# PE fillers on a tile of ones written by DVE, and the fp32 identity copied by DVE instead of ACT

## The chip, the cores and the metric

The kernel runs on one core of a Trainium2 chip. A core has a matrix engine (PE, TensorE), with its weight loads (PEld) shown apart, a vector engine (DVE), a scalar engine (ACT), a general engine (POOL), which also issues most loads here, and a queue engine (SP), which issues the stores. Each engine runs its own instructions in order and waits for others by semaphores. The metric is the device time of one execution in microseconds; the median of several runs is compared.

## What is computed

Chunked attention, followed by a two-layer network with a leaky ReLU, over 8 batches, 8 heads, 576 positions and a head size of 64:

```python
chunk = 64
scores = scale * np.matmul(q_c, k_c.transpose(0, 1, 2, 4, 3))   # per chunk of 64
scores = scores - np.max(scores, axis=-1, keepdims=True)
attn = np.exp(scores)
attn = attn / (np.sum(attn, axis=-1, keepdims=True) + 1e-09)
out = np.matmul(attn, v_c)
...
x = np.ascontiguousarray(attn_out.transpose(0, 2, 1, 3)).reshape(B * S, H * D)   # 4608 x 512
h = x @ w_in                    # 512 -> 2048
g = np.maximum(0.01 * h, h)
out = (g @ w_out)               # 2048 -> 512, float32
```

Inputs and output are fp32 in memory; the kernel computes its matmuls in fp16, but for the first transposes.

## The kernel before

Work is cut into units of 128 token positions (two chunks), 36 in all; unit u covers 8 heads at once. For a unit, the stages have one letter each: `tq` and `tk` transpose queries and keys on PE into PSUM (L259), `q` and `k` copy them to SBUF (L272 or L274 into the tile QZ, which holds the two head halves in zeroed blocks; L279 or L281 into KT), `s` computes the scores (L309), `m` and `b` find and subtract the maximum (DVE), `x` takes the exponential (ACT, L328), `z` and `n` sum and normalise (DVE), `e` transposes the result on PE (L351), `c` copies it, `v` multiplies by the values (L376) with the tile VB, whose unused blocks are zeroed, and `a` stores the unit's 512 features per token in xT (ACT, L389). From unit 9 on, transposes are done by DVE and by DMA instead.

The network takes xT in blocks of tokens (BLOCKS, L46; the first six are of 128). First layer: `mm1` (L157) and ACT's `act1` (L172); second layer: `mm2` (L182), ACT's copy (L193) and a store from SP (L195).

The order of everything is the order of the program text, which each engine follows for its own instructions. Up to unit 5 it is a list written out by hand, FRONT (L431), whose words name a stage and its arguments. Besides the stages above, its words are `y` (DVE zeroes a QZ tile, 0 to 2, or one half of a VB tile, from 3 up, L417), `w` (ACT zeroes a VB half in two steps, L424), `I` (the identity is copied to fp32, L410), `i` with a number (that many filler matmuls, whose results nobody reads, into a PSUM tile of the matmul pool, L396), `A`, `G`, `B`, `O` (first layer, its activation, second layer, store, of the first blocks). After FRONT a loop (L473) runs the stages of unit `it` and its neighbours between `fill` calls, which take matmuls of the network from a list.

Loads are issued up front by POOL in the order of LOADS (L133): `g` are a unit's queries and keys (L69), `v` values (L96), `Q` quarters of the first weights (L103), `P` quarters of the second (L115), `D` a whole batch of queries and keys for the later units (L87). POOL makes the fp16 identity after the first of these, `g1` (a memset and a select, masks.py:197 and 199). The queries and keys of unit 0, q_f and k_f, are loaded in fp32 by SP and ACT (L123). They are fp32 in SBUF, so unit 0's two transposes use the fp32 identity, `ident32`; all others use the fp16 `ident`. Each DMA load is spread over 16 DMA engines, and PE, in order, cannot pass a transpose whose load hasn't landed.

DVE's first writes are two columns, `one` (which ACT reads for a first exponential behind its table load, L127) and `zeros` (which ACT's zeroing reads).

Of the kernel before, what the change touches and what calls it, by code (L numbers as in the profile page):

```python
# [8 lines left out]
FP16 = mybir.dt.float16  # L9
FP32 = mybir.dt.float32  # L10
ALU = mybir.AluOpType
AFT = mybir.ActivationFunctionType
# [4 lines left out]
def kernel(  # L17
# [9 lines left out]
    nc = tc.nc  # L27
# [20 lines left out]
    sbp = ctx.enter_context(tc.tile_pool(name="k_sb", bufs=1))  # L48
# [72 lines left out]
    for eng, name, src in ((nc.sync, "q_f", q), (nc.scalar, "k_f", k)):  # L121
        t = sbp.tile([128, H, D], FP32, name=name)
        eng.dma_start(out=t, in_=src[0, :, 0:G, :].rearrange("h p d -> p h d"))  # L123
        first.append(t)
    one = sbp.tile([128, 1], FP16, name="one")
    nc.vector.memset(one, 0.0)
    nc.scalar.activation(out=one, in_=one, func=AFT.Exp, bias=0.0, scale=1.0)  # L127
# [8 lines left out]
    ident = sbp.tile([128, 128], FP16, name="ident")  # L136
# [4 lines left out]
    ident32 = sbp.tile([128, 128], FP32, name="ident32")  # L141
# [251 lines left out]
    def idle(n):  # L393
        t = psp.tile([128, 4, 128], FP32, name="idle", tag="mm", bufs=4)
        for i in range(n):
            nc.tensor.matmul(out=t[:, i % 4, :], lhsT=ident, rhs=ident, start=True, stop=True)  # L396

    def first_layer(j, a):
        chunks.remove(("mm1", j, a, 0))
# [7 lines left out]
        store(j, 0)  # L407

    def identity():
        nc.scalar.activation(out=ident32, in_=ident, func=AFT.Copy, bias=0.0, scale=1.0)  # L410

    def empty(i):
        i, m = divmod(i, 2)
# [5 lines left out]
    def zero_act(i):  # L419
# [8 lines left out]
            )  # L428

    FRONT = (  # L430
        "y0 y1 y2 y4 w3 I y5 i12 tq0 tk0 q0.1.1 q0.0 tq1 k0.1 q1.0.1 i4 s0 tk1 m0 k1 b0 q1.1.1 i23 s1 x0 "  # L431
        "m1 b1 z0 x1 z1 i55 tq2 q2.0.1 n0 i7 tk2 k2 q2.1 i3 e0 n1 c0.1 s2 m2 i3 v0 a0 b2 i12 e1 x2 c1 i9 "
        "v1 z2 A0.0 a1 A1.0 n2 G0.0 e2 A0.1 c2 v2 tq3 a2 A1.1 q3.1 G0.1 q3.0 tk3 A2.0 G1.0 k3.1 G1.1 s3 "
        "A0.2 G2.0 m3 A1.2 b3 x3 A2.1 G0.2 z3 A0.3 G1.2 tq4 G2.1 n3 A1.3 G0.3 e3 G1.3 A2.2 c3 q4.0.1 v3 "
# [4 lines left out]
        "tq": stage_tq, "tk": stage_tk, "q": stage_q, "k": stage_k, "s": stage_s, "m": stage_m, "b": stage_b,  # L439
        "x": stage_x, "z": stage_z, "n": stage_n, "e": stage_e, "c": stage_c, "v": stage_v, "a": stage_a, "d": stage_d,  # L440
        "A": first_layer, "G": act1, "B": second_layer, "O": finish, "i": idle, "y": zero, "w": zero_act,
        "I": identity,
    }
    done = set()
# [13 lines left out]
    for what in FRONT.split():  # L458
        name = what.rstrip("0123456789.")
# [80 lines left out]
```

## Time and profile before

| What | us |
|---|---|
| median of 3 runs | 293.99 (293.66 to 294.13) |
| the profiled execution, own time | 294.1 |
| its span, first to last instruction | 292.3 |
| PE busy | 284.4 (97%) |
| DVE busy | 182.7 (63%) |
| ACT busy | 152.5 (52%) |
| POOL busy | 119.4 (41%) |
| fillers (L396), 128 matmuls, busy | 9.6 |
| first filler | 3.80 |
| first matmul of the first layer | 18.57 |

The span runs from the first to the last instruction of the program; 1.8 us of the execution's time lie around it. A chain of waits is followed back from the last instruction: at each step to what released it, or else to the instruction before it on its engine. In the timeline each row has start, duration, engine, line, operation, names and shapes, and in brackets the engine's idle time before it and what ended that. In the list of DMA issues the last number is the median time from issue to landing. PE's busy time counts matmuls whose ends are modelled, so two neighbouring rows overlap; the spacing of starts is what one matmul costs in a stream. The page's row of the granted clock shows full speed in all slices.

### The profile page before, as it was taken

The numbers are of one execution on the slowest core, as the hardware profiler recorded it, in microseconds if no ns is written. First come the engines' busy times: TensorE is split into PE (matmuls) and PEld (weight loads), VectorE is DVE, ScalarE is ACT, GpSimd is POOL, SyncE is SP. The second block draws the span as 40 slices with busy tenths as digits, with TensorE's granted clock in tenths as the row PEclk, the third lists the DMA queues.
The fourth block names the chain that finished last, engine by engine and source line by source line (L and its number), as shares of the span: only waits on it lengthen the run. The fifth ranks groups of instructions, "written<-read, shape, count | busy, mean of one in ns | idle before, by whom it ended". The sixth has DMA issues, their size and how long they took to land.

```text
span 292.3 us, 6210 instructions
## 1 busy us (share of the span) xinstructions
PE 284.4 (97%) x2556; PEld 181.8 (62%) x2556; DVE 182.7 (63%) x338; ACT 152.5 (52%) x270; POOL 119.4 (41%) x148
## 2 busy tenths in 40 slices
PE   4999999999999999999999999999999999999995
PEld 3989955878677766767676754444454444444444
DVE  5776536879899898888877888787777720000000
ACT  5457713756456545646454547733763387127511
POOL 8857547898509837920394379210000000000000
PEclk9999999999999999999999999999999999999999
DMA  9999999999999999999499999992111320120022
GB/s 131 162 193 194 202 157 184 168 144 146 127 126 61 148 147 135 139 132 99 66 135 138 105 85 148 94 137 90 56 23 31 112 69 0 38 88 21 0 74 72
DMA packets 192332, 32.00 MB, mean 109 GB/s; under 512 B 183472, under 2 KB 187824, under 8 KB 192304
## 3 DMA queue, kind: packets, MB, share of 16 engines
q0 software_dynamic: 170208, 18.10, 114.0%
q1 hardware_dynamic: 21056, 13.24, 19.4%
q8 instruction: 20, 0.33, 0.4%
q10 hardware_dynamic: 1040, 0.26, 0.4%
q14 instruction: 8, 0.07, 0.1%
HBM read 36.70 MB, written 9.44 MB: 158 GB/s over the span
## 4 chain that ended last, share of the span: by engine, by line
PE 97%; POOL 1%; ACT 1%; issue 1%; DVE 0%; POOLq 0%
PE hT L157 43%; PE oP L182 41%; PE Sp L309 3%; PE xp L376 3%; PE idle L396 3%; PE oP L203 1%; PE qp L259 1%; PE tpe L351 1%; PE kp L259 1%; POOL k_in L69 0%; DVE QZ L274 0%; ACT KT L281 0%; ACT QZ L272 0%; POOL q_in L69 0%; ACT osb L211 0%
## 5 line engine op out<-in xcount | busy, mean ns | idle before, releaser
L157 PE MATMUL hT<-xT,w_inT 128*128 128x128 f16 (+2 forms) x1152 | 134.3, 273 | 0.0
L182 PE MATMUL oP<-w_outT,gT 128*128 128x512 f16 x560 | 128.2, 379 | 0.0
L157 PEld LDWEIGHTS <-w_inT 128*128 128x128 f16 x1152 | 90.0, 98 | 32.7
L172 ACT ACTIVATE gT<-hT 128x512 f16<-128x512 f32 x144 | 83.8, 597 | 32.5 <-PE hT L157 32.3
L182 PEld LDWEIGHTS <-gT 128*128 128x128 f16 x560 | 52.3, 98 | 56.3
L193 ACT ACTIVATE osb<-oP 128x512 f32<-128x512 f32 x35 | 20.9, 596 | 64.6 <-PE oP L182 62.7
L87 POOL DMA_DIRECT2D q_d<-in_q_dram x48 | 38.7, 818 | 35.3 <-DVE QZ L291 31.6
L318 DVE TENSOR_REDUCE mx<-Sp 128x8 f32<-128x512 f32 x36 | 24.9, 691 | 31.0 <-PE Sp L309 30.8
L87 POOL DMA_DIRECT2D k_d<-in_k_dram x48 | 38.7, 817 | 2.1 <-DMA q_d<-in_q_dram 1.1
L291 DVE STREAM_TRANSPOSE QZ<-q_d 64x512 f16<-64x512 f16 (+1 forms) x60 | 38.2, 644 | 0.4
L389 ACT ACTIVATE xT<-xp 128x512 f16<-128x512 f32 x36 | 21.4, 594 | 20.6 <-PE xp L376 20.6
L96 POOL DMA_DIRECT2D VB<-in_v_dram x16 | 18.4, 1159 | 20.8 <-PE xp L376 20.5
L334 DVE TENSOR_REDUCE z<-ex 128x8 f32<-128x512 f16 x36 | 23.6, 654 | 4.7 <-ACT ex L328 4.6
L322 DVE TENSOR_TENSOR sh<-Sp,mx 128x512 f32<-128x512 f32 x36 | 24.9, 691 | 1.2
L343 DVE TENSOR_TENSOR en<-ex,zi 128x512 f16<-128x512 f16 x36 | 24.8, 690 | 1.2
L328 ACT ACTIVATE ex<-sh 128x512 f16<-128x512 f32 x36 | 22.6, 628 | 5.3 <-DVE sh L322 5.3
L299 DVE STREAM_TRANSPOSE KT<-k_d 128x512 f16<-128x512 f16 (+1 forms) x30 | 19.4, 654 | 0.8
L376 PEld LDWEIGHTS <-VB 128*128 128x128 f16 x288 | 13.1, 98 | 5.6
L309 PEld LDWEIGHTS <-QZ 128*128 128x128 f16 x288 | 13.2, 99 | 5.4 <-DVE QZ L274 0.2
L309 PE MATMUL Sp<-KT,QZ 128*128 128x64 f16 x288 | 14.5, 195 | 0.1
L376 PE MATMUL xp<-et,VB 128*128 128x64 f16 x288 | 14.3, 193 | 0.0
L396 PE MATMUL idle<-ident 128*128 128x128 f16 x128 | 9.6, 233 | 3.8 <-POOL ident masks.py:199 3.8
(42 smaller groups left out, 104.2 us busy)
## 6 DMA issues: line engine op xcount, KB each, us to landing
out_dram<-osb SPq DMA_DIRECT2D x35, 256.0 KB, 2.3
VB<-in_v_dram POOLq DMA_DIRECT2D x16, 288.0 KB, 6.0
q_d<-in_q_dram POOLq DMA_DIRECT2D x48, 72.0 KB, 6.0
k_d<-in_k_dram POOLq DMA_DIRECT2D x48, 72.0 KB, 5.3
w_inT<-in_moe_w_in_dram POOLq DMA_DIRECT2D x8, 256.0 KB, 9.2
w_outT<-in_moe_w_out_dram POOLq DMA_DIRECT2D x4, 512.0 KB, 9.5
q_in<-in_q_dram POOLq DMA_DIRECT2D x7, 128.0 KB, 9.7
k_in<-in_k_dram POOLq DMA_DIRECT2D x7, 128.0 KB, 9.0
```

The costliest lines, as they stand in the source:

```text
L87: nc.gpsimd.dma_start(out=t[p0:p0 + 32, m, :, :, :].rearrange("p h b d -> p (h b) d"), in_=src[b, h0:h0 + 2, :, dh * 32:dh * 32 + 32].rear ...
L157: nc.tensor.matmul(out=hT[:, i, :], lhsT=w_inT[:, t, fc * 128:(fc + 1) * 128], rhs=xT[:, t, r0:r0 + tb], start=(t == 0), stop=(t == NT - 1),)
L172: nc.scalar.activation(out=gT[j][:, nf * a:nf * a + nf, :], in_=HT.pop((j, a)), func=AFT.Prelu, bias=0.0, scale=1.0, alpha=0.01)
L182: nc.tensor.matmul(out=o, lhsT=gT[j][:, fc, ti * 128:(ti + 1) * 128], rhs=w_outT[:, fc, :], start=(n == 0 and fc == part * 4), stop=(n == ...
L291: nc.vector.transpose(out=qz[s * CH:(s + 1) * CH, :, e0:e0 + n, s, :], in_=qkd[b][0][s * CH:(s + 1) * CH, :, at:at + n * CH].rearrange("p ...
L309: nc.tensor.matmul(out=Sp[:, i, :], lhsT=qz[:, 2 * m + g, e, :, :], rhs=kt[:, 2 * m + g, e, :], start=True, stop=True)
L318: nc.vector.tensor_reduce(out=MX[u], in_=SP[u], axis=AXL.X, op=ALU.max)
L322: nc.vector.tensor_tensor(out=SH[u], in0=SP.pop(u), in1=MX.pop(u).unsqueeze(2).to_broadcast((128, 8, CH)), op=ALU.subtract)
L328: nc.scalar.activation(out=E[u], in_=SH.pop(u), func=AFT.Exp, bias=0.0, scale=SCL)
L334: nc.vector.tensor_reduce(out=z, in_=E[u], axis=AXL.X, op=ALU.add)
L343: nc.vector.tensor_tensor(out=E[u], in0=ex, in1=ZI.pop(u).unsqueeze(2).to_broadcast((128, 8, CH)), op=ALU.mult)
L376: nc.tensor.matmul(out=xp[:, t, e, :], lhsT=VB[b % NVB][:, t, c, :], rhs=et[:, t // 2, e, t % 2, :] if u < UD else et[:, t % 2, e, t // 2, :],
```

## The change

A new fp16 tile of 128x128, `warm`, is set to 1.0 by DVE before its other writes, and all fillers use it as weights and as data. The list FRONT begins with 33 fillers; the 12 that stood behind `y5` are gone, the others stay. The copy of the identity to fp32 is done by DVE, behind `y4`, and ACT's zeroing `w3` follows it in the list.

```diff
+    warm = sbp.tile([128, 128], FP16, name="warm")
+    nc.vector.memset(warm, 1.0)
     one = sbp.tile([128, 1], FP16, name="one")
     nc.vector.memset(one, 0.0)
     nc.scalar.activation(out=one, in_=one, func=AFT.Exp, bias=0.0, scale=1.0)
...
     def idle(n):
         t = psp.tile([128, 4, 128], FP32, name="idle", tag="mm", bufs=4)
         for i in range(n):
-            nc.tensor.matmul(out=t[:, i % 4, :], lhsT=ident, rhs=ident, start=True, stop=True)
+            nc.tensor.matmul(out=t[:, i % 4, :], lhsT=warm, rhs=warm, start=True, stop=True)
...
     def identity():
-        nc.scalar.activation(out=ident32, in_=ident, func=AFT.Copy, bias=0.0, scale=1.0)
+        nc.vector.tensor_copy(out=ident32, in_=ident)
...
     FRONT = (
-        "y0 y1 y2 y4 w3 I y5 i12 tq0 tk0 q0.1.1 q0.0 tq1 k0.1 q1.0.1 i4 s0 tk1 m0 k1 b0 q1.1.1 i23 s1 x0 "
+        "i33 y0 y1 y2 y4 I w3 y5 tq0 tk0 q0.1.1 q0.0 tq1 k0.1 q1.0.1 i4 s0 tk1 m0 k1 b0 q1.1.1 i23 s1 x0 "
```

On DVE the order is then `warm`, `one`, `zeros`, three QZ tiles, a VB half, the identity's copy, a VB half, and from there as before. On ACT the copy is missing and the rest stands as it was. PE has 21 weight loads and 21 matmuls more, all at its head.

## The prediction

> **What bounds the kernel now.** I read the page first, then the chain of waits from 0 to 60 us, the waits of PE, the timeline of the first 27 us and of 40.5 to 47.5 us, and the landings of single loads. Times are microseconds from the start of the span.
>
> ```profile
> PE 97%; POOL 1%; ACT 1%; issue 1%; DVE 0%; POOLq 0%
> ```
>
> The chain that ended last is PE almost throughout. The chain of the front shows what fills it before the first layer starts at 18.5:
>
> ```profile
> 3.80 1.46 PE idle L396 x12
> 5.26 0.98 PE qp L259 x4
> 6.24 0.02 issue
> 6.26 0.60 ACT QZ L272
> 6.86 0.02 issue
> 6.88 0.69 DVE QZ L274
> 7.58 0.04 issue
> 7.62 0.59 PE qp L259 x4
> 8.20 0.43 PE idle L396 x4
> 8.63 0.43 PE Sp L309 x8
> 9.06 0.43 PE kp L259 x4
> 9.48 1.39 PE idle L396 x23
> 10.87 0.31 PE Sp L309 x8
> 11.18 3.07 PE idle L396 x55
> ```
>
> Two things are to be seen. First, the start hangs on the identity, and then on its fp32 copy behind ACT's zeroing. Second, the same filler costs 0.43/4 = 0.107 us at 8.2 but 3.07/55 = 0.056 us at 11.2: PE runs at half rate at first. Single matmuls in the trace change spacing at 9.55. From 18.3 on no PE gap exceeds 0.02 us, so a microsecond saved before 18.5 is saved at the end, unless something that PE does not pace is late. In the timeline:
>
> ```profile
> 2.82 1.02 DVE L417 MEMSET VB<- 64x1152 uint32 x1 [0.28 <-issue]
> ...
> 3.45 0.29 POOL masks.py:199 TENSOR_SCALAR_AFFINE_SELECT ident<-ident 128x128 f16<-128x128 f16 x1
> ...
> 4.76 0.29 ACT L410 ACTIVATE ident<-ident 128x128 f32<-128x128 f16 x1
> ```
>
> The order there is POOL's identity, DVE's zeroing of one VB half, ACT's copy of the identity. Later, from the other timeline:
>
> ```profile
> 46.74 0.27 PEld L259 LDWEIGHTS <-k_in 128*128 128x128 f16 x4
> ```
>
> That is the weight load of unit 6's keys. The transfer that brings them was issued at 32.83, and that of the first queries, q_f, at 0.74; the last column is the time from issue to landing:
>
> ```profile
> k_in<-in_k_dram POOLq DMA_DIRECT2D x1, 128.0 KB, 13.5
> ```
>
> ```profile
> q_f<-in_q_dram SPq DMA_DIRECT2D x1, 256.0 KB, 3.9
> ```
>
> So q_f lands at 4.61 and unit 6's keys at 46.33, 0.41 before PE uses them.
>
> **The change part by part.**
>
> *The ones tile.* DVE's first write, now 128x128 fp16. Bounds: 0.06 (the 128x1 memset) and 0.49 (one QZ memset, 128x512 uint32); linear in elements between them gives 0.17. It starts at 0.81 and ends at 0.98, and PE may start at 1.04 (the first filler followed the identity by 0.06). What stands behind it on DVE moves by 0.17: `one` is awaited by ACT only after its table load at 2.54, and the zeroed QZ tiles not before 5.8, so this costs nothing.
>
> *Fillers 12 to 33.* At half rate 33 x 0.107 = 3.52: from 1.04 to 4.56. Before, twelve ended issuing at 5.05. The other fillers keep number and cost, and read ones instead of the identity.
>
> *The fp32 copy.* ACT loses 0.29. DVE does it after the VB memset, which now ends at 3.84 + 0.17 = 4.01; the identity is there at 3.74. The price on DVE isn't in the trace: at least 0.17 (128x8 fp32 TENSOR_SCALAR), at most 0.67 (128x512 cast of KT from fp32); I take 0.30, nearest to ACT's 0.29 for this very tile. It is ready at about 4.35, by the bounds 4.2 to 4.75. Behind it waits the second VB memset, which now ends near 5.6; DVE next works at 6.4. Nothing waits. No DMA is added; POOL's and SP's queues keep their order, and POOL's loads to unit 8 wait for other loads only.
>
> *The first transpose* then waits for the latest of fillers (4.56), copy (4.41 with 0.06 to start) and q_f (4.61 + 0.06 = 4.67). So it starts at 4.67 instead of 5.11: 0.44 gained, set by q_f. With the copy at 0.67 the gain is 0.3.
>
> *Full rate earlier.* Before, it took 9.55 - 3.80 = 5.75 from the first filler. The same interval from 1.04 gives 6.8. The chain from first transpose to the second pair's (L259 at 7.62) took 2.51, in ACT and DVE mostly, so that pair comes at 7.18, already at full rate. Step by step: KT's copy ends at 8.17 - 0.44 = 7.73, and s0 starts at 7.78 (before 8.42, held back by four slow fillers). Eight Sp and four kp matmuls then need 0.62 instead of 1.06, so kp is done at 8.40. ACT's KT (0.60) and QZ half (0.59) end at 9.64, and s1 starts at 9.69 instead of 10.77: 1.08 gained. The 23 fillers end at 9.52 and don't hold it. The 55 fillers at 0.056 follow unchanged, and q2's transposes come at 13.0 instead of 14.09 (their data lands at 12.12; the keys, at 13.23, are used at 13.57).
>
> By the Trainium skill ("TensorE: Matmul & The Clock Gate", "PE-mode transpose") a transpose doesn't count as PE being busy in the way that releases the clock. By its section on the clock gate a window lasts 3.4 us; the one before the switch at 9.55 held some twelve transposes of 0.11 to 0.21 us and only seven fillers and eight Sp, so this trace speaks against it; what it would do here is the third rival.
>
> *Where the 1.08 goes.* These loads are not paced by PE. First-layer quarters land at 16.22, 18.95, 23.16 and 25.72 against uses at 18.54, 20.70, 24.32 and 27.1: all still in time, the third by 0.08. Unit 5's keys (40.33, used 41.3) allow 0.9. Unit 6's keys allow least: a landing at 46.33, 0.06 to start, a use at 46.74, so 0.35. PE executes in order; if it arrives 1.08 early it stands at 45.7 and waits 0.7 for the keys. Later units land over 4 us before use.
>
> Sum: 1.08 gained before 18.5, 0.73 lost again at 46, net 0.35. On the profiled execution's 294.1 that is 293.75, and on the median of 293.99, 293.64; I forecast 293.65.
>
> **The rivals.**
>
> *The wait at unit 6 is not there (faster).* By the completion marks of that load in the trace, fifteen of 16 DMA engines were done by 44.86 and one at 46.33. If the straggler is an accident of this execution, keys land at 45.4 or earlier, and the next limit is unit 5's 0.9 or all of the 1.08: 293.0 to 293.2, say 293.1. Against it: the same lag of one engine is there for every load from 38.6 on, so it isn't one load's chance.
>
> *The keys come later still (slower).* PE's code comes in packets on a queue of its own; one stands in this stretch of 49.8 to 49.9:
>
> ```profile
> q8 instruction: 1, 0.02, 60.9%
> ```
>
> Each takes one DMA engine for about 0.95 (60.9% of 16 engines in 0.1), and the page has 0.33 MB in 20 packets for 5112 PE rows, one per 256 rows. Four have passed before the keys land and the fifth starts at 49.86, about 5 after PE passed row 1152. The change puts 42 rows in front (21 weight loads, 21 matmuls); that row is reached 2.8 earlier by row count (42.0 instead of 44.8), and 1.08 more by the gain: the fifth starts near 46.0. It decides from the point where it precedes the keys' last bytes on the engine that is last anyway: then keys land at 47.28, PE starts at 47.34 instead of 46.74, and the kernel is 0.6 slower than before, 294.6. Against it: successive code packets seem to strike different engines, as the number of lagging ones grows with each.
>
> *The early fillers don't release the clock.* Full rate only at 9.55 as before: s0 at 8.03 by four slow fillers, and the 23 fillers end at 10.48, so s1 gains 0.3; 293.7. That the change does not do what it says (PE's first instruction late, q_f late) ends between this and 294.0.
>
> **How the numbers follow.** Chances: the forecast 0.42; no wait at unit 6 0.32; keys later 0.16; no early release, or no gain, 0.10. About 0.2%, 0.59 us, is what a measurement of this kernel can tell from no change. The forecast lies within it, but its size hangs on one landing after 43 us of saturated loading; if that shifts earlier by 0.25, it is over the bound, to which I give 0.15 of the 0.42. Faster: 0.32 + 0.15 = 0.47. Same: 0.27 + 0.10 = 0.37. Slower: 0.16. The forecast's own range is 293.2 to 294.0; with the others, 292.8 to 294.6.
>
> **What would show it.** Right: PE's first filler near 1.0; the first transpose near 4.67, released by q_f's load rather than by the copy; spacing of 0.056 before 7.2; s1 near 9.7; the first layer from about 17.5; and a PE wait of some 0.7 near 46 ended by k_in's load. No wait there, with the end about 1 us earlier, shows the first rival; a wait of over 1.5, with a code packet just before, the second; 0.107 spacing at 9.3 the third. The forecast is wrong if PE waits for the copy or for code, or if the span does not follow from the start of the first layer less the waits for loads.

## The result, and the profile after

| | before | changed |
|---|---|---|
| median of 22 runs, us | 293.75 (293.51 to 294.41) | 293.33 (293.08 to 293.62) |
| ratio to before, 95% | | 0.9983 (0.9976 to 0.9989) |
| the profiled execution, own time | 294.1 | 293.59 |
| its span | 292.3 | 291.8 |
| first transpose | 5.11 | 4.92 |
| full rate from | 9.57 | 5.02 |
| scores of unit 1 (`s1`) | 10.78 | 9.60 |
| first layer from | 18.57 | 17.39 |

The kernel is faster by 0.17%, within the 0.2% that was called no change. ("Full rate from" is read from the spacing of single matmul starts in the trace.) The profiled execution of before took 0.35 more than the median of its runs, so the two traces lie further apart than the medians, by 0.51 instead of 0.42. Line numbers are two higher than before.

The chain that ended last, its first line on the page:

```profile
PE 96%; DVE 1%; ACT 1%; issue 0%
```

The same chain over the first 13 us (start, duration, what; x is the number of instructions):

```profile
2.92 1.02 DVE VB L419
...
3.97 0.91 DVE ident L412
4.88 0.04 issue
4.92 0.70 PE qp L261 x4
5.62 0.02 issue
5.64 0.60 ACT QZ L274
6.24 0.02 issue
6.27 0.69 DVE QZ L276
6.96 0.14 issue
7.10 0.38 PE qp L261 x4
7.48 0.22 PE idle L398 x4
7.70 0.29 PE Sp L311 x8
7.99 0.22 PE kp L261 x4
8.22 1.28 PE idle L398 x23
9.50 0.09 issue
9.60 0.39 PE Sp L311 x8
```

The first four transposes cost 0.70 here against 0.98 before, four fillers 0.22 against 0.43: full rate has come. What holds the first transpose, by this chain, is DVE's copy, 0.91 long, and DVE's chain ahead of it. The timeline shows what else runs then (start, duration, engine, line, operation; in brackets the idle time before and its end):

```profile
1.06 3.70 PE L398 MATMUL idle<-warm 128*128 128x128 f16 x33 [1.06 <-DVE zeros L131]
3.69 2.31 POOL L96 DMA_DIRECT2D VB<-in_v_dram  x2
3.97 0.89 DVE L412 CAST ident<-ident 128x128 f32<-128x128 f16 x1
4.38 1.02 DVE L419 MEMSET VB<- 64x1152 uint32 x1
```

The 33 fillers run from 1.06 and are done before the copy is. POOL writes a load of values while DVE copies; the first of its two instructions there ends at 4.85, the copy 0.02 later.

The first transpose also needs q_f, which was issued at 0.74; the list of DMA issues:

```profile
q_f<-in_q_dram SPq DMA_DIRECT2D x1, 256.0 KB, 4.0
```

It landed at 4.79. In the four traces below in which q_f comes last, the first transpose begins 0.135 behind its landing (`early_copy`, `early_a21`, `both_free`, `no_head_fillers`); in the four in which DVE's copy comes last, it begins 0.055 behind the copy's end (`a21_first`, `wide_fillers`, `loads_free`, `change_again`). Either gives 4.92 here, so in this trace the two tie, though the chain names only the copy.

The first layer starts 1.18 earlier than before, yet the span is only 0.51 shorter. The rest is lost at one place. The timeline around 23 us:

```profile
23.13 0.60 ACT L174 ACTIVATE gT<-hT 128x512 f16<-128x512 f32 x1 [0.17 <-PE hT L159]
...
23.83 1.33 PE L159 MATMUL hT<-xT,w_inT 128*128 128x128 f16 x21 [0.51 <-ACT gT L174]
```

PE stands still ahead of block 0's third first-layer piece (`A0.2`). The trace names ACT's activation, which ended at 23.73. But that piece also needs the third quarter of the first weights, whose second half was issued at 13.18; the list of DMA issues of that moment, with the time to landing last:

```profile
w_inT<-in_moe_w_in_dram POOLq DMA_DIRECT2D x1, 256.0 KB, 10.6
```

It landed at 23.74; before, at 23.16. A second profiled execution of the same kernel (`change_again`, below) tells the two releasers apart. Its timeline at that place:

```profile
23.58 0.60 ACT L174 ACTIVATE gT<-hT 128x512 f16<-128x512 f32 x1 [0.17 <-PE hT L159]
23.61 2.06 PE L159 MATMUL hT<-xT,w_inT 128*128 128x128 f16 x34
```

There the quarter was in at 23.36, and PE went on at 23.61 while the same activation ran until 24.18. So the piece doesn't wait for that activation; it was the load. The load cost 0.67, all of it at this piece: the 0.51 in the bracket counts from a modelled end, and by the starts of single matmuls, set against `change_again`, everything from this piece on is 0.67 later and nothing else is lost. PE's last second-layer matmul comes 270.73 after the first layer's start, instead of 270.06.

### The profile page after: what moved, and what is told of

It is laid out like the page before. It is cut to its first block, busy times and chain, and to the rows that moved or that the text cites. A ratio compares the mean times of both kernels' runs of the same rounds, so it can differ in the third digit from the quotient of the medians.

```text
span 291.8 us, 6254 instructions
## 1 busy us (share of the span) xinstructions
PE 285.5 (98%) x2577; PEld 182.5 (63%) x2577; DVE 183.9 (63%) x340; ACT 152.4 (52%) x269; POOL 119.5 (41%) x148
## 3 DMA queue, kind: packets, MB, share of 16 engines
HBM read 36.70 MB, written 9.44 MB: 158 GB/s over the span
## 4 chain that ended last, share of the span: by engine, by line
PE 96%; DVE 1%; ACT 1%; issue 0%
PE hT L159 43%; PE oP L184 41%; PE xp L378 3%; PE Sp L311 3%; PE idle L398 2%; PE oP L205 1%; PE qp L261 1%; PE tpe L353 1%; PE kp L261 1%; DVE QZ L419 0%; DVE VB L419 0%; DVE ident L412 0%; DVE QZ L276 0%; ACT gT L174 0%; ACT KT L283 0%
## 5 line engine op out<-in xcount | busy, mean ns | idle before, releaser
L345 DVE TENSOR_TENSOR en<-ex,zi 128x512 f16<-128x512 f16 x36 | 24.9, 690 | 1.2
L398 PE MATMUL idle<-warm 128*128 128x128 f16 x149 | 11.5, 239 | 1.1 <-DVE zeros L131 1.1
```

The source lines that it names most:

```text
L345: nc.vector.tensor_tensor(out=E[u], in0=ex, in1=ZI.pop(u).unsqueeze(2).to_broadcast((128, 8, CH)), op=ALU.mult)
```

## The experiments

Twelve kernels ran in four groups, each group on one chip with its own runs of the kernel before. Two theories are set against each other. L: the early start is worth 1.1 to 1.2, and loads that PE does not pace eat part of it. Its rival P: what is gained depends on the moment at which the clock is released, which differs from execution to execution. Edits are shown against the changed kernel. This table has what each profiled execution shows, in us from the start of its span; "later" is the time from the first layer's start to the last second-layer matmul.

| kernel | first transpose | full rate from | s1 | first layer | later | its time | median | ratio to before (95%) |
|---|---|---|---|---|---|---|---|---|
| before | 5.11 | 9.57 | 10.78 | 18.57 | 270.06 | 294.10 | 293.75 | |
| changed | 4.92 | 5.02 | 9.60 | 17.39 | 270.73 | 293.59 | 293.33 | 0.9983 (0.9976, 0.9989) |
| a21_first | 4.91 | 6.19 | 10.02 | 17.80 | 270.06 | 293.34 | 293.37 | 0.9984 (0.9974, 0.9993) |
| wide_fillers | 4.92 | 3.80 | 9.56 | 17.67 | 270.06 | 293.24 | 293.35 | 0.9984 (0.9975, 0.9992) |
| warm_only | 5.11 | 5.17 | 9.77 | 17.55 | 270.22 | 293.26 | 293.45 | 0.9988 (0.9979, 0.9996) |
| copy_only | 5.04 | 9.58 | 10.66 | 18.52 | 270.07 | 294.06 | 293.76 | 0.9995 (0.9986, 1.0004) |
| loads_free | 4.92 | 4.69 | 9.57 | 17.35 | 270.06 | 292.89 | 293.39 | 0.9980 (0.9971, 0.9988) |
| early_copy | 4.82 | 4.83 | 9.44 | 17.22 | 270.12 | 292.82 | 293.31 | 0.9983 (0.9974, 0.9992) |
| no_head_fillers | 4.95 | 11.80 | 11.64 | 19.66 | 270.38 | 295.52 | 294.71 | 1.0023 (1.0010, 1.0037) |
| both_free | 4.95 | 7.04 | 10.02 | 17.80 | 270.65 | 293.93 | 293.19 | 0.9981 (0.9973, 0.9990) |
| late_free | 8.38 | 9.03 | 13.29 | 21.07 | 270.06 | 296.61 | 296.76 | 1.0096 (1.0083, 1.0109) |
| late_fixed | 8.54 | 5.68 | 13.14 | 20.99 | 270.37 | 296.84 | 297.72 | 1.0137 (1.0122, 1.0151) |
| change_again | 4.91 | 6.89 | 10.02 | 17.83 | 270.06 | 293.38 | 293.36 | 0.9992 (0.9979, 1.0005) |
| early_a21 | 4.80 | 4.58 | 9.41 | 17.19 | 270.07 | 292.73 | 293.12 | 0.9978 (0.9969, 0.9987) |

In each of them the profiled time is the first layer's start plus "later" plus 5.48 (5.47 to 5.51): a microsecond ahead of the first layer, or in a wait behind it, is a microsecond of the whole.

**a21_first.** The pieces that need the third quarter later come first; `A2.1`, which needs the second, moves ahead of `A0.2`.

```diff
-        "A0.2 G2.0 m3 A1.2 b3 x3 A2.1 G0.2 z3 A0.3 G1.2 tq4 G2.1 n3 ...
+        "A2.1 G2.0 m3 A0.2 b3 x3 A1.2 G2.1 z3 A0.3 G0.2 tq4 G1.2 n3 ...
```

> The changed kernel, with the first-layer piece A2.1 (third quarter-free: it needs weights that landed long ago) put ahead of A0.2 and A1.2, which read the third quarter of the first weights; same matmuls, other order, so A0.2 comes 0.9 us later. Theory L (PE's gain of about 1.2 us before the first layer is cut to 0.5 by one late load, the third quarter, landing at 23.74): the PE gap of 0.51 us ahead of A0.2 goes, and the kernel takes 292.7 to 292.95, about 0.4 us less than the change alone, unless unit 5's or 6's keys are late next. Rival O (that gap is only where a lag made elsewhere shows, by ACT's activation as the page names it): the gap moves but stays about 0.5, and the time is 293.3.

PE waited for no load and the gap is gone, as theory L has it and against rival O, but the first layer began at 17.80 instead of 17.39: full rate came only at 6.19, after the first transposes, and s1 at 10.02. So time 293.34 and median 293.37, above the 292.7 to 292.95 of theory L: nothing gained over the change. Seven of its eleven runs lie between 293.34 and 293.40, beside this trace's time. Taking the wait away and the later release came together in this execution, and neither theory is excluded by it.

**wide_fillers.** Four fillers become one over 512 columns (the data is the tile of ones four times over), so 50 matmuls do for the 149 fillers, and its code packets come later.

```diff
-        for i in range(n):
-            nc.tensor.matmul(out=t[:, i % 4, :], lhsT=warm, rhs=warm, start=True, stop=True)
+        wide = warm.unsqueeze(1).to_broadcast((128, 4, 128))
+        for i in range(n // 4):
+            nc.tensor.matmul(out=t, lhsT=warm, rhs=wide, start=True, stop=True)
+        for i in range(n % 4):
+            nc.tensor.matmul(out=t[:, i, :], lhsT=warm, rhs=warm, start=True, stop=True)
```

> The changed kernel, with fillers of 512 moving columns (the ones read four times) instead of four of 128: same PE time, about 200 fewer rows in PE's program by the first layer. Theory C (the second code packet, moved from 22.1 to 21.3 us by 42 more rows, takes one DMA engine for 1.2 us ahead of the third quarter's end and makes it land at 23.74 instead of 23.16): only one code packet before 23 us instead of two, the quarter lands at 23.2 or before, the gap ahead of A0.2 is 0.1 at most, and the kernel takes 292.8 to 293.0. Rival D (the landing differs from run to run without the code): two landings near 23.2 to 23.7 as before, time 293.1 to 293.4.

One code packet (19.05) instead of two came ahead of 23 us; the quarter landed at 22.96 and PE did not wait. That is what a packet delaying the load would give. But `change_again` has the changed kernel's packets and its quarter came at 23.36, `a21_first` at 22.30, again without a wait. Landings differ by that much anyway, so the packet is not shown to be the cause. The gain of 0.67 was partly lost to something new, 0.45 of PE's time at 14.4. The timeline a little earlier shows its start:

```profile
11.68 0.89 POOL L69 DMA_DIRECT2D k_in<-in_k_dram  x1 [0.55 <-DMA VB<-in_v_dram]
12.04 0.49 DVE L338 TENSOR_SCALAR ze<-z 128x8 f32<-128x8 f32 x1
12.57 0.20 DVE L340 RECIPROCAL zi<-ze 128x8 f32<-128x8 f32 x1
```

The small TENSOR_SCALAR takes 0.49 beside POOL's issue of keys, which a wait had put 0.28 later than in the changed kernel; its twin at 13.36 takes 0.17. DVE is behind, and PE waits for its normalised result (L345). The first layer starts 0.28 later than in the change.

**warm_only.** Early fillers alone: the fp32 copy goes back to ACT, behind its zeroing.

```diff
     def identity():
-        nc.vector.tensor_copy(out=ident32, in_=ident)
+        nc.scalar.activation(out=ident32, in_=ident, func=AFT.Copy, bias=0.0, scale=1.0)
...
-        "i33 y0 y1 y2 y4 I w3 y5 tq0 ...
+        "i33 y0 y1 y2 y4 w3 I y5 tq0 ...
```

> The changed kernel with the identity's fp32 copy back on ACT behind its zeroing: only the fillers differ from the kernel before. By theory L the full clock by itself brings nearly all: first transpose at 5.1, at full rate; second scores (s1) near 9.8 instead of 10.77 before, the first layer from 17.6, then cut by the third quarter's load: 293.2 to 293.4, the same as the change. If the copy mattered, 293.5 to 293.7.

The first layer starts 1.02 earlier than before, at 17.55, with the first transpose where it was. So nearly all of the change's start comes from the fillers, in these two traces. The median, 293.45, lies between the two ranges that were expected. Here the third quarter was in at 23.17, and the wait that the prediction named, for unit 6's keys, is there. Its timeline:

```profile
45.56 0.39 PE L261 MATMUL qp<-ident,q_in 128*128 128x128 f16 x4
45.92 0.23 PEld L261 LDWEIGHTS <-k_in 128*128 128x128 f16 x4 [0.15 <-DMA k_in<-in_k_dram]
```

The keys landed at 45.88 and PE lost 0.16.

**copy_only.** The other half: fillers as before, on the identity, and only the copy on DVE.

```diff
-    warm = sbp.tile([128, 128], FP16, name="warm")
-    nc.vector.memset(warm, 1.0)
...
-            nc.tensor.matmul(out=t[:, i % 4, :], lhsT=warm, rhs=warm, start=True, stop=True)
+            nc.tensor.matmul(out=t[:, i % 4, :], lhsT=ident, rhs=ident, start=True, stop=True)
...
-        "i33 y0 y1 y2 y4 I w3 y5 tq0 ...
+        "y0 y1 y2 y4 I w3 y5 i12 tq0 ...
```

> The kernel before with only the identity's copy moved to DVE; fillers on the identity, twelve behind y5 as before. The copy takes 0.89 us on DVE by the profile of the change, so it ends near 4.75, but the twelve fillers hold PE to 5.05: nothing is gained, the first transpose stays at 5.0 to 5.1, at half rate, 293.6 to 293.9. If the copy matters, first transpose 0.1 to 0.3 earlier and 293.4 to 293.6.

It moves the first layer by 0.05, and its median can't be told from the kernel before. The copy itself shows something else. The timeline:

```profile
3.69 2.35 POOL L96 DMA_DIRECT2D VB<-in_v_dram  x2
3.87 0.23 DVE L410 CAST ident<-ident 128x128 f32<-128x128 f16 x1
```

Without the memset of ones DVE is 0.10 earlier, and the same copy takes 0.23 instead of 0.89.

**loads_free.** `a21_first` and, for unit 6's keys, one load of values moved behind them, and one piece of the second layer ahead of unit 5's transposes.

```diff
-        "g1 v0 g2 Q0 Q1 g3 Q2 Q3 g4 P0 P1 P2 P3 g5 v1 g6 g7 g8 D2 "
+        "g1 v0 g2 Q0 Q1 g3 Q2 Q3 g4 P0 P1 P2 P3 g5 g6 v1 g7 g8 D2 "
...
-        "B0.0 z4 B1.1 n4 B3.0 B1.2 B0.3 tk5 tq5 k5.1 B0.2 q5.1.1 e4 ...
+        "B0.0 z4 B1.1 n4 B3.0 B1.2 B0.3 B0.2 tk5 tq5 k5.1 q5.1.1 e4 ...
```

> The changed kernel with three places made indifferent to when loads land: A2.1 ahead of A0.2 (0.9 us more for the third quarter), unit 6's queries and keys loaded ahead of the second batch's values (some 4 us earlier), unit 5's transposes one second-layer piece (0.9 us) later. Theory L (loads cut the gain, a different one from run to run; a21_first freed only one of three): no PE gap after 18 us, and what is gained at the first layer, 0.8 to 1.2 us, stays to the end: median 292.8 to 293.1. Rival P (loads bind only now and then; the time when the clock is released decides, run by run, how much is gained at the first layer): median within 0.1 of the 293.35 of a21_first.

The profiled execution is theory L's: release at 4.69, first layer at 17.35, no wait, 292.89. Its median, 293.39, is not: if loads were what held most runs back, it would have dropped well below the change's 293.33. It lies where P put it.

**early_copy.** The copy comes ahead of DVE's VB zeroing, as soon as the identity is there; the second VB zeroing goes far back, where DVE has time.

```diff
-        "i33 y0 y1 y2 y4 I w3 y5 tq0 ...
+        "i33 y0 y1 y2 I y4 w3 tq0 ...
...
-        "B0.0 z4 B1.1 n4 B3.0 ...
+        "B0.0 z4 B1.1 n4 y5 B3.0 ...
```

> The changed kernel with the identity's copy put ahead of y4 on DVE, and y5 moved back to behind n4. Theory S (the copy's 0.89 us is not its own work: it meets POOL's descriptor writing for the values, issued at 3.69, and ends 0.02 us after that instruction; in copy_only it began 0.1 us earlier and took 0.23): the copy begins at about 3.78, takes 0.23, and the first transpose starts at 4.6 to 4.7, held by fillers or q_f, instead of 4.92; the first layer comes 0.2 to 0.3 earlier, the time 293.1 to 293.35. Rival T (0.89 is what the copy costs here): it ends near 4.7 and the first transpose gains at most 0.2.

The timeline:

```profile
3.68 2.30 POOL L96 DMA_DIRECT2D VB<-in_v_dram  x2
3.76 0.23 DVE L412 CAST ident<-ident 128x128 f32<-128x128 f16 x1 [1.12 <-POOL ident masks.py:199]
...
4.82 0.63 PE L261 MATMUL qp<-ident,q_f 128*128 128x128 f32 x4
```

The copy takes 0.23 and is over at 3.99, as theory S has it. The first transpose now waits for q_f, which landed at 4.68, 0.135 ahead of it; the last filler had started at 4.45. So it comes at 4.82, later than the 4.6 to 4.7 that was expected and 0.10 earlier than in the change, where q_f itself landed 0.10 later. s1 is 0.16 earlier, and the time 292.82. The median, 293.31, does not follow.

**no_head_fillers.** The change without its 33 first fillers.

```diff
-        "i33 y0 y1 y2 y4 I w3 y5 tq0 ...
+        "y0 y1 y2 y4 I w3 y5 tq0 ...
```

> The changed kernel without the 33 fillers at the head; the copy and all else as changed. Theory K (the fillers act by releasing the clock early): the first transpose starts at 4.9 as in the change, but at half rate (0.21 us each), full rate comes at 8 to 11.7 instead of 3.8 to 6.2, the first layer at 18.3 to 19, the time 293.6 to 294.3, no better than before. If the start time is what counts: 293.4.

PE's timeline, two rows of transposes and one of fillers:

```profile
4.95 1.09 PE L261 MATMUL qp<-ident,q_f 128*128 128x128 f32 x4 [4.95 <-DVE ident L412]
...
7.53 0.58 PE L261 MATMUL qp<-ident,q_in 128*128 128x128 f16 x4 [0.64 <-DVE QZ L276]
7.91 0.63 PE L398 MATMUL idle<-warm 128*128 128x128 f16 x4
```

Half rate until 11.80, the first layer at 19.66, and a kernel slower than before by 0.23% (0.10 to 0.37). The first transpose comes at 4.95, about as in the change (q_f landed at 4.82), so it is the rate that is missing, and with it over 2 us. Its runs form two groups, 293.75 to 293.96 (five) and 294.53 to 295.52 (seven), and the trace is of the second; an earlier release would explain the first, but no trace shows it.

**both_free.** `loads_free` and `early_copy` together (both diffs above).

> loads_free and early_copy together. Theory L with S: first transpose at 4.6 to 4.7, s1 at 9.3 to 9.8, no PE gap after 18 us, 292.6 to 292.9. By P: 293.1 to 293.3.

In this execution q_f itself came late (4.81), the release at 7.04, and the loads late too. PE's waits (what it did, what it waited for: total, times, longest):

```profile
PE hT L159 <- DMA w_inT<-in_moe_w_in_dram: 0.2, 1, 0.2
PE qp L261 <- DMA q_f<-in_q_dram: 0.2, 1, 0.2
```

The third quarter landed at 24.02 and the fourth's halves at 25.30 and 26.58, although the order was made to bear lateness. By the starts of single matmuls PE lost 0.41 at the last of these, which the list shows as 0.2, and 0.14 at unit 4's queries (landed at 27.61), 0.59 in all with a small remainder. The median is 293.19, in P's range and above L's, the profiled run 293.93: one execution says little about a kernel whose runs spread over 0.8.

**late_free and late_fixed.** Both delay the whole start by some 3.5, so that every load is in long before it is needed; then what still spreads is not loads. The first lets PE begin late, by six memsets of DVE ahead of the ones. The second keeps PE's begin and holds the first transpose back by a filler that waits for fourteen memsets.

```diff
     warm = sbp.tile([128, 128], FP16, name="warm")
+    pad = sbp.tile([128, 1024], FP16, name="pad")
+    for _ in range(6):
+        nc.vector.memset(pad, 0.0)
     nc.vector.memset(warm, 1.0)
...
-        "i33 y0 y1 y2 y4 I w3 y5 tq0 ...
+        "i33 y0 y1 y2 y4 I w3 tq0 ...
```

> The changed kernel with six writes of an unused tile ahead of the ones tile on DVE (about 3.2 us), and y5 behind n4: PE's start and all that follows come about 3 us later while the loads do not, so no load can hold PE, but the clock's release still falls where it falls. Rival P (the release sets the spread): the first transpose near 7.8 to 8.4, no PE gap after 18 us, and runs still spread over 0.5 us or more. Theory L (loads set the spread): runs within 0.3 us. Median 295.6 to 296.5 by both.

```diff
+    gate = sbp.tile([128, 128], FP16, name="gate")
...
+    def gated(n):
+        for i in range(n):
+            nc.vector.memset(gate, float(i % 2))
+        t = psp.tile([128, 4, 128], FP32, name="idle", tag="mm", bufs=4)
+        nc.tensor.matmul(out=t[:, 0, :], lhsT=gate, rhs=gate, start=True, stop=True)
...
-        "i33 y0 y1 y2 y4 I w3 y5 tq0 ...
+        "i60 y0 y1 y2 I y4 w3 g14 tq0 ...
```

> The changed kernel with 60 fillers at its head and then one filler on a tile that DVE finishes writing near 7.7 us (14 small writes behind y4; the copy ahead of y4, y5 behind n4): the first transpose starts near 7.8 in all runs, after the clock has been released in all (latest release seen with early fillers 7.04), and no load can hold PE. By P and by L: no PE gap after 18 us and runs within 0.3 us, at 295.6 to 296.1 (292.8 plus the delay). If the spread stays 0.5 or more, neither the release nor the loads make it.

In both, `y5` stands behind `n4` as in `early_copy`. Runs of `late_free` still spread by 0.96 (296.05 to 297.01, five runs) with "later" at its floor of 270.06, which speaks for P. But `late_fixed`, whose first transpose comes at 8.54, behind the latest release seen with early fillers (7.04), spreads by 1.28 (296.84 to 298.12, four runs), which neither theory has. By the starts of single matmuls its profiled execution lost 0.21 at 31.7 to DVE's normalised result and 0.11 at 83.8 to a DMA transpose, 0.31 in all. A delayed start shifts DVE and the transposes against the loads, and new collisions come. The pair doesn't separate the theories.

**change_again.** The changed kernel unaltered, for a second profile.

> The changed kernel once more, for another trace. By both: the last second-layer matmul ends 270.06 us after the first layer's start plus what PE waits for loads; the waits differ from the first trace's 0.67. By P the release lies between 3.4 and 7.2 and the first layer at 17.35 to 17.4 if it comes by 5, 17.8 if near 6.2 to 7.

It lost nothing to loads (270.06) and still needs 293.38, since its release came at 6.89. The chain and PE's timeline agree on what that costs; from the timeline:

```profile
4.91 1.12 PE L261 MATMUL qp<-ident,q_f 128*128 128x128 f32 x4
...
7.52 0.38 PE L261 MATMUL qp<-ident,q_in 128*128 128x128 f16 x4 [0.64 <-DVE QZ L276]
...
10.02 0.39 PE L311 MATMUL Sp<-KT,QZ 128*128 128x64 f16 x8
```

The first four transposes at half rate take 1.12 instead of 0.68, and everything behind is 0.42 later: s1 at 10.02 instead of 9.60. So two executions of one kernel end within 0.21 of each other by different ways: one starts the first layer at 17.39 and loses 0.67 to a load, the other starts at 17.83 and loses none. The copy held the first transpose here: it ended at 4.86, and q_f had been there since 4.55. Two of the twelve runs took 294.62 and 295.01, and against the runs of its own group the kernel can't be told from before (0.9979 to 1.0005).

**early_a21.** `early_copy` and `a21_first` together, as a version that may beat both.

> The changed kernel with the copy ahead of y4 (as in early_copy) and A2.1 ahead of A0.2 (as in a21_first). By the traces so far the first layer starts 17.2 if the clock is released by about 5, 17.6 to 17.7 if later, and the last second-layer matmul comes 270.06 after it when no load is waited for: span 291.05 or 291.45, times 292.8 or 293.2, median 293.0 to 293.2, against 293.33 to 293.36 of the change. If the copy's 0.1 to 0.2 is lost to loads again, 293.3.

Release at 4.58, s1 at 9.41, no load waited for, 292.73; median 293.12. It is the best of the kernels that ran by its ratio, 0.9978. Against the change's 0.9983 that is about 0.15 us, with intervals that overlap and on another chip: likely, not shown.

## Why the prediction was right, and where not

**PE from 1.04, ones tile 0.17.** Right: the tile took 0.17, the first filler came at 1.06. In all kernels with early fillers they were over before the first transpose could start.

**The fp32 copy, 0.30 within 0.17 to 0.67.** Wrong, and outside its bounds: 0.89. The nearest row, ACT's copy of this tile, gave a fair price of the work (0.23 measured when free), but the step left out POOL, which was writing a load at the time. Six traces have the copy beginning at 3.97, 0.28 to 0.29 after POOL's instruction began, and 0.89 to 0.90 long; six have it beginning 0.07 to 0.19 after, and 0.23 long. The sum had the copy as hidden behind q_f; in four traces it is what sets the first transpose, and in the recorded one it ties with q_f. So one sign that the prediction gave for being wrong, PE waiting for the copy, did appear.

**First transpose at 4.67, set by q_f.** Wrong by 0.25, for two reasons that tie in the recorded trace. The copy ended at 4.87. And q_f would have given 4.92 by itself: it landed at 4.79 instead of 4.61, and the transpose begins 0.135 behind a landing of q_f, not 0.06. With the copy out of the way q_f sets it, as forecast: 4.82 in `early_copy`, 4.80 in `early_a21`, 4.95 in `both_free`. Landings of q_f lie between 4.33 and 4.82 in the 14 traces.

**Full rate near 6.8, s1 at 9.69.** The interval of 5.75 from the first filler was taken for a constant, and it isn't: releases in the nine traces whose first filler comes at 1.06 and whose start isn't held back on purpose lie between 3.80 and 7.04. s1 came at 9.60, near the forecast, by two errors that cancel, which is luck: the first transpose came 0.25 later, and transposes at full rate gained 0.42. With a release after the first transposes the prediction's own chain gives 9.69 + 0.25 = 9.94, and `change_again`, `a21_first` and `both_free` have 10.02. Those two plateaus, 9.4 to 9.8 and 10.02, are what the release's moment decides here. That it is decided from execution to execution agrees with the Trainium skill ("TensorE: Matmul & The Clock Gate", "Part 1: The HAM clock gate"), by which the activity is watched in free-running windows of 3.4 us: the spread of 3.24 fits into one.

**Early fillers release the clock (third rival).** Decided for the forecast by `warm_only`, `copy_only` and `no_head_fillers`: the gain is theirs. Whether transposes count as busy at all, the rule named there, no run settles: in `no_head_fillers` full rate came at 11.80, behind transposes, but behind 27 later fillers too.

**1.08 gained ahead of the first layer.** Right in size: 1.18 in the recorded trace; 0.74 in the one with a late release.

**PE then waits 0.73 for unit 6's keys.** The kind of loss was right and its size close, the place wrong. In the recorded trace it was the third first-layer quarter, 0.67, for which the prediction had a margin of 0.08 and which it called "still in time". The keys' load, in the ten traces with POOL's order as it was, took 12.1 to 12.6 from issue to landing in eight, 13.4 in `warm_only`, where they cost 0.16, and 13.5 before: the straggler comes in some executions and not in others, as the first rival allowed. In the recorded trace they landed at 45.28 and nothing waited for them, so that rival's condition held, but not its time. The step that failed is the reading of one execution's landings as fixed: the third quarter came between 22.30 and 24.02 in the traces whose start isn't held back, at 23.36 and 23.74 in two executions of the changed kernel, and a margin of 0.08 was no margin.

**Rival 2, a code packet that delays a load.** The fifth packet, which it named, came at 47.70 instead of near 46.0, when unit 6's keys had long landed. The second did come earlier too (21.33 instead of 22.11, and the third quarter landed late behind it), but `change_again` with the same packets had its quarter in time. No run was slower for it. Not shown.

**The time.** 293.65 was forecast and 293.33 measured, in the forecast case's own range (293.2 to 294.0). Of the difference, 0.24 is the base: the forecast started from a median of three runs of before, 293.99, and that of 22 is 293.75. The gain was 0.34 by forecast and 0.42 between the medians. The mechanism, a gain of about 1.1 at the start of which about 0.7 is lost to a load, is the recorded trace's, with another load than the one forecast. In `change_again` it is a gain of 0.74 of which nothing is lost. That the net came out near the forecast is in part luck. The start of before isn't fixed either: by the sum under the table, a run of before that takes 293.51 has its first layer at 17.97 at the latest, 0.6 ahead of the trace's 18.57. So the 1.18 is the difference of two executions and not the gain of the median run.

What fixes the median of the runs without a trace is open. If it were loads, `loads_free` should have lowered it, and it didn't; if it were the release, `early_copy` and `loads_free`, which do nothing about it, fit. The medians of `loads_free` and `both_free` came where P put them and not where L did, and the runs of `a21_first` gather at the time of its late release. That points to P, but the pair made to show it did not separate. Both happen in traces; their shares aren't known.

## What to carry to other kernels

Give PE something to multiply from its first microsecond, on a tile that nothing but one early memset provides: it brought the first layer forward by 0.7 and 1.2 us in the two traces of the change, and the median by 0.4, where the real work of the front is a chain of small steps, and twelve of them, begun 2.7 later (`copy_only`), left the clock slow until 9.58. Before moving an operation to DVE, look at what POOL issues at that moment, not only at DVE's own queue. Take a load's landing from several executions before calling a margin of less than a microsecond safe or short.

## What the runs showed of the hardware

**A copy on DVE that begins inside POOL's load issue, but not in its first 0.2 us, ends with it.** 128x128, fp16 to fp32: 0.227 us where it isn't held, 0.89 when begun 0.28 to 0.29 after the start of POOL's 1.16 us instruction, and then over 0.02 after that one's end. Begun within 0.19 of its start, it isn't held, also in `late_free` beside another load's issue (7.80 against 7.73). The small TENSOR_SCALARs of all 14 traces show the same. The 213 that begin outside POOL's issues take 0.17, and so do the 24 that begin in the first 0.22 us of one. Of the 251 that begin later than 0.24 us into one, none ends more than 0.04 ahead of the issue's end, even if that makes it 0.90 long. The one that took 0.49 in `wide_fillers` is of these; so is one in the changed kernel that began 0.67 into the same issue of keys, where its own 0.17 already brings it to the end. By the Trainium skill ("SBUF — State Buffer", "Who interferes with whom") DVE's copy, cast and tensor_scalar can need a port pair that GpSimd shares, and whoever comes first holds it to its end. The long copies agree. Two things in the runs don't follow from it: what begins in the first 0.2 us of an issue isn't held; and in the changed kernel the memset behind the copy was recorded from 4.38 with its usual 1.02, 0.41 after the copy's start as in `copy_only`, while the copy was still held.

**The release of the clock wanders over one kernel's executions**: 5.02 and 6.89 in two of the changed kernel, 4.58 to 7.04 in the eight traces with the same 33 fillers from 1.06, 3.80 in the one with wide fillers. Here that is worth 0.42 us of the total, or nothing, by whether the first fp32 transposes fall ahead of it.

**The same load's time to landing differs between traces by more than a microsecond**: unit 6's keys took 12.1 to 13.5, the third quarter's second half 9.6 before and 10.6 in the change. Two executions of the changed kernel differ less, by 0.05 and 0.3 for these two. What lags was not looked into beyond the code packets above.
